# A linear-attention layer and a Fourier-mixing layer in one kernel: the transform in four groups, rows only centred by their sum, the state held in PSUM over three chunks, and the order of all operations given as a table

## The chip, the cores and the metric

The kernel runs on one core of a Trainium2 chip. The metric is the device time of one execution in microseconds. The core has five engines that run side by side, each through its own list of instructions in order: TensorE (PE in the profile, its weight loads PEld), VectorE (DVE), ScalarE (ACT), GpSimd (POOL) and SyncE (SP, which here only starts DMAs). An engine that meets an instruction whose input is not there waits, and everything behind that instruction waits too.

## The reference

There are 4 batches, 8 heads, 768 time steps and a head size of 48, so a row is 8 x 48 = 384 wide.

```python
for t in range(S):                                   # attention with a decaying state
    y[t]  = r[t] . (state + (u * k[t]) v[t]^T)
    state = w * state + k[t] v[t]^T
X = real(fft(fft(x, axis=1), axis=2))                # over 768 steps, then over 384 columns
u = x + X
un = (u - mean(u)) / sqrt(var(u) + 1e-6)             # per row
out = u + relu(un @ w1) @ w2                         # 384 -> 1536 -> 384
```

## The kernel before, in words

The 24 **chunks** (4 batches of 6) have 128 time steps each. For a chunk, SP starts three loads (`k` and `r` into the two halves of `kr`, L306 and L309; `v` into `vt`, L313). DVE scales `k` and `r` by tables of powers of `w` into `KR` (L329), ACT casts `v` to `V` (L334), PE turns `KR` by eight transposes (`tp`, L339), ACT copies that to `KRT` (L342), DVE makes the products `PR` (L343). PE computes the scores `A_ps` (L353); they are masked to `MA` either by ACT (copy `AC`, L365) and POOL (L367) or by DVE alone (L360). The **state** update is PE's `u_ps` (L381): four products of `KR` and `V`, and from the second chunk of a batch on one more product with the identity that adds the previous state `Sst` (L384); DVE multiplies it by `w` to the 128th power, `WD`, into the next `Sst` (L388). The chunk's output gathers in `yd_ps` (L403, L408, L423); the term with `u` goes through ACT (`DE`, L413) and POOL (`TT`, L414), and DVE adds both into the batch's rows `X` (L427).

When a batch's six chunks are there, DVE **folds** it: sums and differences of the two halves of the sequence (`EO`, L445) and of the two halves of the row (`XF`, L451). PE multiplies by the tables of the first transform (L475: 18 products, 384 or 386 columns wide, in six accumulations), ACT copies the result to `TT` (L482; the trace calls it TT as well), DVE copies it reversed to `TR` (L491), which serves the other half of the frequencies. The second transform (L510, L512, L514) takes for each of six blocks of 128 rows six products: two of 384 and four of 192 columns. DVE adds `X` into `UF` (L520), takes each row's mean and variance (L525, L527), ACT and DVE turn these into `rstd` and `nm` (L536 to L540), and ACT writes the normed row `UN` (L545). `UN` is turned into `UNT`, in batch 0 by PE and DVE (L566, L569), in the others by a transposing DMA. The two-layer product follows for each half batch: 12 groups of 3 matmuls (L594) with a relu on ACT into `HT` (L598), then for each block 12 matmuls (L610), and DVE adds `UF` into `osb` (L617), which POOL sends out (L620).

The order in which each engine meets its work is made by a planner in the kernel's Python: every operation is recorded with an engine and a duration in `op`, and `order` starts again and again the operation that can begin first. What comes out is a fixed list for each engine. Until a planned time `WARM` it also puts in products with a tile of zeros (L626), which compute nothing that is used. Tables for the transforms come over SP's queue (`te`, `to`, `hid`, L296), the weights `W1`, `W2` over POOL's (L648).

Of the kernel before, what the change touches and what calls it, by code (L numbers as in the profile page):

```python
# [15 lines left out]
B = 4  # L16
# [7 lines left out]
NP = H // 2  # L24


def _tables():

    bf = mybir.dt.np(BF16)
    n = np.arange(384)  # L30
    ke = np.arange(0, 385, 2)
    ko = np.arange(1, 384, 2)

    def seq(k):
        a = 2.0 * np.pi * np.outer(n, k) / S
        t = np.concatenate([np.cos(a), np.sin(a)], axis=1)
        return t.reshape(3, 128, -1).transpose(1, 0, 2)

    te = seq(ke)
    to = seq(ko)  # L40
    te[:, :, 193] = 0.0
    te[:, :, 385] = 0.0
    d = np.arange(192)
    le = np.arange(0, 384, 2)
    lo = np.arange(1, 384, 2)
    hid = []
    for f, sg in ((np.cos, 1.0), (np.sin, -1.0), (np.sin, 1.0)):
        e = sg * f(2.0 * np.pi * np.outer(d, le) / DM)
        o = sg * f(2.0 * np.pi * np.outer(d, lo) / DM)
        t = np.zeros((128, 768))  # L50
        t[:, 0:192] = e[0:128]
        t[0:64, 192:384] = e[128:192]
        t[64:128, 384:576] = o[0:64]
        t[:, 576:768] = o[64:192]
        hid.append(t)
    hid = np.stack(hid, axis=1)
    mtri = np.triu(np.ones((128, 128)), 1)
    ident = np.eye(128)
    return [np.ascontiguousarray(x.astype(bf)) for x in (te, to, hid, mtri, ident)]


class _Tile:


    def __init__(self, source, ring, bufs):
        self.source, self.ring, self.bufs = source, ring, bufs
        self.ops = []
        self.value = None
# [5 lines left out]
class _Schedule:  # L74

    LATENCY = 80  # L80
    LANDING = 1900
    COLD = 8000

    def __init__(self):
        self.ops, self.made, self.at = [], {}, {}
# [4 lines left out]
    def given(self, name, at):  # L90
        self.at[name] = at

    def op(self, eng, ns, fn, r=(), w=(), new=(), use=(), after=(), dma=0, pri=0, until=None):
        o = dict(eng=eng, ns=ns, fn=fn, deps=list(r), after=list(after), w=list(w), new=list(new), dma=dma, pri=pri, until=until,
                 n=len(self.ops))
        for t in set(new) | set(use):
            t.ops.append(o)
        self.ops.append(o)

    def order(self):  # L100
        makes = {}
        for o in self.ops:
            for k in o["w"]:
                makes[k] = o
        users = {}
        for o in self.ops:
            srcs = {makes[k]["n"] for k in o["deps"] if k in makes}
            behind = {makes[k]["n"] for k in o["after"]} - srcs
            o["left"] = len(srcs) + len(behind)
            o["ready"] = max([0] + [self.at[k] for k in o["deps"] if k in self.at])  # L110
            for n in srcs:
                users.setdefault(n, []).append((o, True))
            for n in behind:
                users.setdefault(n, []).append((o, False))
        free, rings, dma_free, done = {}, {}, 0.0, []
        cand = {}
        for o in self.ops:
            if o["left"] == 0:
                cand.setdefault(o["eng"], []).append(o)

        def room(o):
            t = 0.0
            taken = {}
            for tl in o["new"]:
                ring = rings.setdefault(tl.ring, [])
                n = len(ring) + taken.get(tl.ring, 0) - tl.bufs
                taken[tl.ring] = taken.get(tl.ring, 0) + 1
                if n >= 0:
                    if n >= len(ring):
                        return None  # L130
                    for p in ring[n].ops:
                        if "end" not in p:
                            return None
                        t = max(t, p["end"])
            return t

        total = sum(o["until"] is None for o in self.ops)
        while sum(o["until"] is None for o in done) < total:
            best = None
            for e, ops in cand.items():  # L140
                at = free.get(e, 0.0)
                pick = None
                ops[:] = [o for o in ops if o["until"] is None or at < o["until"]]
                for o in ops:
                    t = room(o)
                    if t is None:
                        continue
                    start = max(at, o["ready"], t + self.LATENCY)
                    key = (start, o["pri"], o["n"])
                    if pick is None or key < pick[0]:  # L150
                        pick = (key, o)
                if pick and (best is None or pick[0] < best[0]):
                    best = pick
            assert best, "no operation can start"
# [35 lines left out]
def kernel(  # L190
# [272 lines left out]
    def fourier(b):  # L463
# [22 lines left out]
        for cb in range(3):  # L486
            for par in range(2):
                first(cb, par)
# [208 lines left out]
```

## Time and profile before

| | |
|---|---|
| time, median of 3 runs | 205.12 us (205.09 to 205.95) |
| profiled execution, its own time | 207.08 us |
| span of the profile, first to last instruction | 205.4 us |
| PE busy / DVE / ACT / POOL | 186.4 / 137.8 / 128.8 / 62.9 us |
| granted TensorE clock, mean | 0.968 |
| filler products with zeros (L626) | 79 in the trace, 21.9 us busy |
| first matmul of the two-layer product (L594) | at 56.81 us |
| last matmul | ends at 200.1 us |

Busy time counts a matmul from its issue to its modelled end; matmuls overlap, so the pace of a run of them is read from their starts. Idle time of an engine costs nothing by itself; what matters is which wait ends last in a stage.

### The profile page before, as it was taken

How to read it: one execution, taken by the hardware profiler on the slowest of the kernel's cores; microseconds unless marked ns; L12 is line 12 of the kernel's file. 1: busy time of each engine (PE TensorE's matmuls, PEld its weight loads, DVE VectorE, ACT ScalarE, POOL GpSimd, SP SyncE). 2: the span in 40 equal slices, each digit the busy share in tenths (PEclk: the TensorE clock that was granted, in tenths of full speed). 3: DMA queues.
4: the chain of work that ended last, by engine and by line, in shares of the span. 5: the costliest groups of instructions: out<-in, count | busy, mean ns of one | idle time of the engine just before them, and what ended most of it. 6: DMA issues, size and time to landing. Idle time of an engine off the chain costs nothing.

```text
span 205.4 us, 4458 instructions
## 1 busy us (share of the span) xinstructions
PE 186.4 (91%) x1737; PEld 117.8 (57%) x1738; DVE 137.8 (67%) x281; ACT 128.8 (63%) x260; POOL 62.9 (31%) x92
## 2 busy tenths in 40 slices
PE   7499955599989997999999999999999999999990
PEld 2256632267566664675677677666657665656650
DVE  5278993859899869998999998983645822111220
ACT  2588640563779795759489895996465585664300
POOL 5035974123023442221456321135311012011131
PEclk9999996759999999999999999999999999999997
DMA  4999999999999769561999200144111045111121
GB/s 100 174 185 172 174 290 256 169 190 182 184 201 169 151 135 202 128 118 38 165 234 204 57 3 0 41 96 96 41 38 38 5 97 130 41 66 53 38 87 66
DMA packets 86549, 24.74 MB, mean 120 GB/s; under 512 B 82944, under 2 KB 84608, under 8 KB 86528
## 3 DMA queue, kind: packets, MB, share of 16 engines
q1 hardware_dynamic: 81664, 16.98, 46.6%
q0 software_dynamic: 3680, 7.08, 13.5%
q10 hardware_dynamic: 1184, 0.39, 0.9%
q8 instruction: 13, 0.21, 0.4%
q14 instruction: 8, 0.07, 0.1%
HBM read 20.32 MB, written 4.72 MB: 122 GB/s over the span
## 4 chain that ended last, share of the span: by engine, by line
PE 41%; issue 25%; DVE 11%; DMA 7%; SPq 7%; POOL 4%; ACT 1%; POOLq 0%; DVEq 0%; ACTq 0%
PE mm L594 9%; PE mm L610 8%; DMA kr<-in_r_dram 7%; PE mm L475 4%; PE tp L339 4%; DVE KR L329 4%; POOL out_dram L620 4%; PE mm L510 3%; PE A_ps L353 2%; PE mm L626 2%; SPq L296 2%; PE mm L514 1%; PE mm L512 1%; PE yd_ps L423 1%; SPq L306 1%
## 5 line engine op out<-in xcount | busy, mean ns | idle before, releaser
L598 ACT ACTIVATE HT<-mm 128x384 bf16<-128x384 f32 x96 | 45.3, 495 | 20.4 <-PE mm L594 20.3
L594 PE MATMUL mm<-UNT,W 128*128 128x384 bf16 x288 | 53.2, 326 | 0.1
L610 PE MATMUL mm<-W,HT 128*128 128x384 bf16 x288 | 50.6, 326 | 0.0
L610 PEld LDWEIGHTS <-HT 128*128 128x128 bf16 x288 | 27.7, 98 | 18.3 <-issue 0.3
L594 PEld LDWEIGHTS <-W 128*128 128x128 bf16 x288 | 26.8, 98 | 16.1 <-issue 0.2
L617 DVE TENSOR_TENSOR osb<-mm,UF 128x384 f32<-128x384 f32 x24 | 13.3, 556 | 32.7 <-PE mm L610 32.7
L367 POOL TENSOR_SCALAR_AFFINE_SELECT MA<-AC 128x512 bf16<-128x512 bf16 x29 | 21.6, 750 | 43.9 <-ACT AC L365 33.9
L620 POOL DMA_DIRECT2D out_dram<-osb x24 | 13.4, 559 | 65.5 <-DVE osb L617 52.2
L329 DVE TENSOR_TENSOR KR<-kr,wtab 128x768 bf16<-128x768 f32 x24 | 26.6, 1106 | 9.2 <-DMA kr<-in_r_dram 9.2
L414 POOL TENSOR_TENSOR TT<-V,DE 128x384 bf16<-128x384 bf16 x24 | 21.7, 905 | 28.0 <-ACT DE L413 27.9
L342 ACT COPY KRT<-tp 128x1024 bf16<-128x1024 bf16 x24 | 24.4, 1018 | 4.1 <-PE tp L339 4.0
L626 PE MATMUL mm<-zero 128*128 128x512 bf16 x79 | 21.9, 404 | 1.3 <-DVE icol L267 1.3
L365 ACT CAST AC<-A_ps 128x512 bf16<-128x512 f32 x29 | 16.5, 588 | 7.6 <-PE A_ps L353 7.4
L339 PE MATMUL tp<-ident,KR 128*128 128x128 bf16 x192 | 15.2, 224 | 6.2 <-DVE KR L329 6.0
L334 ACT CAST V<-vt 128x384 bf16<-128x384 f32 x24 | 11.8, 519 | 12.3 <-DMA vt<-in_v_dram 9.0
L339 PEld LDWEIGHTS <-KR 128*128 128x128 bf16 x192 | 11.9, 100 | 11.3 <-DVE KR L329 9.9
L482 ACT CAST TT<-mm 128x386 bf16<-128x386 f32 (+1 forms) x24 | 12.7, 597 | 6.3 <-PE mm L475 6.3
L545 ACT ACTIVATE UN<-UF,nm,rstd 128x384 bf16<-128x384 f32 x24 | 15.3, 697 | 0.9 <-DVE nm L540 0.9
L427 DVE TENSOR_TENSOR X<-yd_ps,TT 128x384 bf16<-128x384 f32 x24 | 13.1, 547 | 3.9 <-POOL TT L414 3.9
L343 DVE TENSOR_TENSOR PR<-KRT 128x512 bf16<-128x512 bf16 x24 | 13.6, 569 | 1.8 <-ACT KRT L342 1.7
L360 DVE TENSOR_TENSOR MA<-A_ps,mtri 128x512 bf16<-128x512 f32 x19 | 12.9, 680 | 2.6 <-PE A_ps L353 2.5
L520 DVE TENSOR_TENSOR UF<-mm,X 128x384 f32<-128x384 f32 x24 | 12.6, 552 | 1.5 <-PE mm L514 0.6
(67 smaller groups left out, 240.0 us busy)
## 6 DMA issues: line engine op xcount, KB each, us to landing
kr<-in_k_dram SPq DMA_DIRECT2D x24, 192.0 KB, 4.8
vt<-in_v_dram SPq DMA_DIRECT2D x24, 192.0 KB, 4.5
out_dram<-osb POOLq DMA_DIRECT2D x24, 192.0 KB, 2.2
kr<-in_r_dram SPq DMA_DIRECT2D x23, 192.0 KB, 4.4
W<-in_moe_w_ch_dram POOLq DMA_DIRECT2D x6, 384.0 KB, 6.7
hid_t<-hid_c SPq DMA_DIRECT2D x1, 576.0 KB, 9.2
te_t<-te_c SPq DMA_DIRECT2D x1, 289.5 KB, 9.2
to_t<-to_c SPq DMA_DIRECT2D x1, 288.0 KB, 8.2
```

What stands on the lines that cost most here:

```text
L329: op("DVE", 960, lambda: nc.vector.tensor_tensor(out=KR().rearrange("t s p (a d) -> t (s p) a d", a=2)[:, :, :, 0:D], in0=kr().rearrange(" ...
L339: nc.tensor.transpose(tp()[:, s, p, :], KR()[:, s, p, :], ident)
L342: op("ACT", 1010, lambda: nc.scalar.copy(KRT(), tp()), r=[("tp", i)], w=[("KRT", i)], new=[KRT], use=[tp], pri=pri)
L365: op("ACT", 590, lambda: nc.scalar.copy(AC(), A_ps[a]()), r=[("A", i)], w=[("AC", i, a)], new=[AC], use=[A_ps[a]], pri=pri)
L367: op("POOL", 680, lambda: nc.gpsimd.affine_select(out=MA[a](), in_=AC(), pattern=[[0, NP], [1, 128]], base=0, channel_multiplier=-1, compa ...
L414: op("POOL", 850, lambda: nc.gpsimd.tensor_tensor(out=TT(), in0=V(), in1=DE().unsqueeze(2).to_broadcast([128, H, D]), op=AluOp.mult), r=[( ...
L545: op("ACT", 705, lambda: nc.scalar.activation(out=UN()[:, j, :], in_=UF()[:, j, :], func=Act.Identity, scale=rstd()[:, j:j + 1], bias=nm() ...
L594: nc.tensor.matmul(hp(), lhsT=W1[:, dt, ft * 128:(ft + 1) * 128], rhs=UNT()[:, :, dt, :], start=(dt == 0), stop=(dt == 2))
L598: op("ACT", 490, lambda: nc.scalar.activation(out=HT()[:, ft, :], in_=hp(), func=Act.Relu), r=[("hp", hf, ft)], w=[("HT", hf, ft)], new=[H ...
L610: nc.tensor.matmul(mo(), lhsT=HT()[:, ft, j * 128:(j + 1) * 128], rhs=W2[:, ft, :], start=(ft == 0), stop=(ft == 11))
L620: op("POOL", 550, lambda: nc.gpsimd.dma_start(out=out[b, row:row + 128, :], in_=osb()), r=[("osb", hf, j)], w=[("out", hf, j)], use=[osb], ...
L626: op("PE", 216, lambda: nc.tensor.matmul(z(), lhsT=zero[:, 0:128], rhs=zero, start=True, stop=True), r=["zero"], w=[("idle", len(sch.ops)) ...
```

## The change

**The first transform in four groups.** The row is folded once more: after `EO` there is a fold of the row's halves (`HH`) and then a fold of each half onto itself reversed (`XF`, now four groups of 97 columns, stored 98 apart). The first transform has four accumulations, one for each group. For batches 1 to 3 each is three pairs of products of 193 columns. Batch 0 skips the fold of the sequence: each chunk is folded by itself (`narrow`), and each group accumulates six pairs as the chunks come, with a table of opposite sign, `tn_t`, which ACT makes from `te_t`. The second transform has four products of 192 columns for a block, with 97 rows of weights.

**Rows only centred.** The add of `X` also gives the row's sum (`sm`). The turned row is `UB`, which is the row's sum less 384 times the row, so minus 384 times the centred row: it waits for the sum and not for the variance. The factor 384 and the sign are taken back by a relu of the negative and by `rstd` computed for the variance times 384 squared; `osb` multiplies by `rstd` at the end. `nm` and the normed row are gone.

**State in PSUM.** `u_ps` stays for three chunks and each adds its products to it; the tables `wtab` have three versions so that no multiplication by a power of `w` falls between. After the third chunk DVE multiplies by `w` to the 384th power, and only the fourth chunk adds an old state by the identity. The other states are plain copies, on DVE (multiplied by a table of ones and zeros) or on ACT (two copies of half the rows each).

**A stored order.** The planner is gone. `ORDER` lists the numbers of the operations as they are issued; a suffix `.1` takes the operation's other form. Such forms exist for copies (ACT or DVE), the masks (ACT and POOL, or DVE), the rows `X` and `UF` (the added tile is put in by PE through the identity, then ACT copies) and the relu (DVE). The numbers given with `op` are not used any more when the kernel is built.

The counts of instructions that change most:

| | before | change |
|---|---|---|
| first transform, PE | 72 of 384 or 386 columns | 120 of 193 |
| second transform, PE | 48 of 384, 96 of 192 | 96 of 192 |
| old state by identity, PE, 384 columns | 16 | 4 |
| `TT`, `X` by identity, PE, 384 columns | none | 9, 16 |
| fillers, PE | 80 | 40 |
| `KRT` copies on ACT / DVE | 24 / 0 | 11 / 13 |
| masks on ACT with POOL / DVE | 29 / 19 | 27 / 21 |
| relu on ACT / DVE | 96 / 0 | 75 / 21 |
| rows `X` on DVE / ACT | 24 / 0 | 15 / 9 |
| states on DVE / ACT | 20 / 0 | 8 / 12 (24 halves) |
| `UF` on DVE / ACT | 24 / 0 | 8 / 16 |
| normed or centred rows on ACT / DVE | 24 / 0 | 10 / 14 |

Where rows move, in three places. First SP's queue at the end of batch 0's loads, where the tables of the transform stand. Before:

```order
L306 DMA kr<-in_k_dram 128x8x48
L313 DMA vt<-in_v_dram 128x8x48
L296 DMA te_t<-te_c 128x1158
L296 DMA to_t<-to_c 128x1152
L296 DMA hid_t<-hid_c 128x2304
L309 DMA kr<-in_r_dram 128x8x48
L313 DMA vt<-in_v_dram 128x8x48
```

In the change:

```order
L274 DMA kr<-in_r_dram 128x8x48 x2
L276 DMA vt<-in_v_dram 128x8x48 x2
L262 DMA te_t<-te_c 128x2316
L262 DMA hid_t<-hid_c 128x1152
L270 DMA kr<-in_k_dram 128x8x48
L274 DMA kr<-in_r_dram 128x8x48
```

`te_t`, now with the contents of both tables, is SP's 20th transfer instead of its 21st; the `k` of chunk 6, which stood ahead of the tables, now follows them with its `r`.

Second, ACT's list in the same stage, from the masks of chunk 4 on. Before:

```order
L365 CAST AC<-A_ps 128x512
L413 COPY DE<-yd_ps 128x8
L334 CAST V<-vt 128x384
L342 COPY KRT<-tp 128x1024
L365 CAST AC<-A_ps 128x512
L482 CAST TT_732<-mm 128x386
```

In the change:

```order
L324 CAST AC<-A_ps 128x512
L661 ACTIVATE tn_t<-te_t 128x1158
L415 CAST X<-yd_ps 128x384
L361 CAST Sst_93<-u_ps 64x4x48 x2
L392 COPY DE<-yd_ps 128x8
L415 CAST X<-yd_ps 128x384
L392 COPY DE<-yd_ps 128x8
```

The making of `tn_t`, which needs `te_t`, stands ahead of the copies of `X` for chunks 3 and 4 and of `DE` for chunks 4 and 5. POOL's first slice of `W1` waits for the `X` of chunk 3, its slices of `W2` for the `X` of chunk 5; before, they followed the issue of loads of chunks 7 to 12.

Third, DVE's list from the transform of batch 0 to the turned rows. Before:

```order
L491 COPY TR<-TT_732 128x768 x3
L329 TENSOR_TENSOR KR_85<-kr,wtab 128x16x48
L520 TENSOR_TENSOR UF<-mm,X 128x2x192 x6
L427 TENSOR_TENSOR X<-yd_ps,TT 128x384
L525 BN_STATS st<-UF 128x6
L527 BN_AGGR MV<-st 128x2
```

In the change:

```order
L306 COPY KRT<-tp 128x1024
L514 COPY TR<-TT_740 97x768 x2
L546 SCALAR_TENSOR_TENSOR UF,sm<-mm,X 128x2x192 x4
L577 COPY UNT<-mm 128x384 x2
L559 TENSOR_SCALAR UB<-UF,sm 128x384 x2
L329 TENSOR_TENSOR MA<-A_ps,mtri 128x512
```

Before, three more pairs of statistics, a reciprocal and `nm` lie between the last row shown and the first `UNT`; in the change two `UNT` follow the four `UF` at once, and the statistics stand behind later chunks.

The diff, cut to its core (`...` marks what is left out):

```diff
+CH = 98
...
-    def order(self):
...
+    def emit(self, order):
         counts = {}
-        for o in self.order():
+        for n, a in order:
+            o = self.ops[n]
...
-            o["fn"]()
+            o["alts"][a][3]()
+
+
+ORDER = """
+154 153 194 150 155 168 157 160 162 195 151 161 159 196 169 177 156 188 199 176 174 197 191 175 163 158 200 178 173 170 171 198 180 172 164 201 179
...
 def attend(i):
...
+            if ph == 0:
+                c["u"] = new(ps, [128, NP, 2, D], F32, "u_ps", 1)
+            else:
+                c["u"] = chk[i - 1]["u"]
...
+            again = q == 3
...
-                                     start=(p == 0), stop=(q == 0 and p == NP - 1), skip_group_check=True)
-                if q > 0:
+                                     start=(ph == 0 and p == 0), stop=(p == NP - 1 and not again), skip_group_check=True)
+                if again:
                     nc.tensor.matmul(u_ps(), lhsT=ident, rhs=S(), start=False, stop=True, skip_group_check=True)
...
+            def halves():
+                for a in range(2):
+                    nc.scalar.copy(Sn()[a * 64:a * 64 + 64, :, a, :], u_ps()[a * 64:a * 64 + 64, :, a, :])
...
+        op(("xt", i), "NONE", 0, lambda: None, r=[("TT", i), ("de", i)], w=[("xt", i)], use=[], pri=pri,
+           other=[("PE", 166, False, lambda: nc.tensor.matmul(
+               yd()[:, 0:DM], lhsT=ident, rhs=TT().rearrange("p h d -> p (h d)"), start=False, stop=False,
+               skip_group_check=True))], fixed=True)
...
+    def narrow(q, pri):
+        X, HH, XF = bat[0]["X"], bat[0]["HH"], bat[0]["XF"]
+        e, n = divmod(q, 3)
...
+        def sym(h, alu):
+            grp = (slice(0, 4, 3), slice(1, 3, 1))[h]
+            op(("XF", 0, q, h), "DVE", 230, lambda: nc.vector.tensor_tensor(
+                out=XF()[:, e, n, 0:4 * CH].rearrange("t (g c) -> t g c", g=4)[:, grp], in0=HH()[:, :, e, n, 0:CH],
+                in1=HH()[:, :, e, n, 192:192 - CH:-1], op=alu),
...
-        def first(cb, par):
...
+        def first(g):
+            fp = new(ps, [128, 2, 193], F32, "mm", 3)
+            last = (NQ if b == 0 else 3) - 1
...
+                for par in range(2):
+                    if b:
+                        lhsT, rhs = XF()[:, par, nb], te_t[:, g % 2, nb, par, :]
...
+                    nc.tensor.matmul(fp()[:, par, :], lhsT=lhsT[:, g * CH:g * CH + 128], rhs=rhs,
+                                     start=(nb == 0 and par == 0), stop=(nb == last and par == 1), skip_group_check=True)
...
             def mm():
...
+                for g in range(4):
+                    lo = j * 128
+                    tb = g if g % 2 == 0 or not sh else 4 + g // 2
+                    nc.tensor.matmul(mp()[:, g // 2, :], lhsT=src()[0:97, g, lo:lo + 128], rhs=hid_t[0:97, tb, :],
+                                     start=(g == 0), stop=(g == 3), skip_group_check=True)
...
+            op(("UF", b, blk), "DVE", 700, lambda: nc.vector.scalar_tensor_tensor(
+                out=parity(UF()[:, j, :]), in0=mp(), scalar=1.0,
+                in1=parity(X()[:, blk, :]), op0=AluOp.mult, op1=AluOp.add,
+                accum_out=sm()[:, j:j + 1]),
...
+               other=[("ACT", 700, False, lambda: nc.scalar.activation(
+                   out=parity(UF()[:, j, :]), in_=mp(), func=Act.Identity, accum_out=sm()[:, j:j + 1]))],
...
+            op(("UB", b, blk), "ACT", 610, lambda: nc.scalar.activation(
+                out=UB()[:, j, :], in_=UF()[:, j, :], func=Act.Identity, scale=-float(DM), bias=sm()[:, j:j + 1]),
...
-        def normed(sh, UF, UNT, MV):
...
-        op("DVE", 555, lambda: nc.vector.tensor_tensor(out=osb(), in0=mo(), in1=UF()[:, j, :], op=AluOp.add),
...
+        op(("osb", hf, j), "DVE", 620, lambda: nc.vector.scalar_tensor_tensor(
+            out=osb(), in0=mo(), scalar=rstd()[:, j:j + 1], in1=UF()[:, j, :], op0=AluOp.mult, op1=AluOp.add),
...
-    table("te", te_t, te_c.ap(), 900)
-    table("to", to_t, to_c.ap(), 900)
-    table("hid", hid_t, hid_c.ap(), 1500)
+    table("te", te_t, te_c.ap(), 1600, 2)
+    table("hid", hid_t, hid_c.ap(), 800, 3)
+    op("tn", "ACT", 1150, lambda: nc.scalar.mul(tn_t, te_t[:, :, :, 1, :], -1.0), r=["te"], w=["tn"], pri=40,
...
+    weights("W1", lambda n: w1[n * 128:(n + 1) * 128, :], lambda n: W1[:, n, :], [("X", 3)], 1870, -90)
```

More of the change, by code (lines that the diff above doesn't have):

```diff
@@ L634 @@
+    MASKED = 3
     prelude()
-    load(0)
-    for i in range(1, NC):
+    table("ident", ident, id_c.ap(), 100, -48)
+    table("mtri", mtri, mtri_c.ap(), 100, -20)
+    for i in range(NC):
         load(i)
-    table("te", te_t, te_c.ap(), 900)
-    table("to", to_t, to_c.ap(), 900)
-    table("hid", hid_t, hid_c.ap(), 1500)
+    table("te", te_t, te_c.ap(), 1600, 2)
+    table("hid", hid_t, hid_c.ap(), 800, 3)
+    op("tn", "ACT", 1150, lambda: nc.scalar.mul(tn_t, te_t[:, :, :, 1, :], -1.0), r=["te"], w=["tn"], pri=40,
+       other=[("DVE", 700, True, lambda: nc.vector.tensor_scalar(
+           out=tn_t, in0=te_t[:, :, :, 1, :], scalar1=-1.0, scalar2=None, op0=AluOp.mult))])
```

570 lines of the change are left out of this document (259 added, 311 removed), and 35 rows, old and new, of the table ORDER.

## The prediction

> **What bounds the kernel now.** I read the page first, for the shares and the slices over the span.
>
> ```profile
> PE 186.4 (91%) x1737; PEld 117.8 (57%) x1738; DVE 137.8 (67%) x281; ACT 128.8 (63%) x260; POOL 62.9 (31%) x92
> DVE  5278993859899869998999998983645822111220
> PEclk9999996759999999999999999999999999999997
> ```
>
> A slice is 5.1 us. PE is busy for most of the span, but DVE is near full in slices 5 to 27, and the granted clock sags in slices 7 to 9, so one share says little. The second view cuts the span at 56.81 us, where the first matmul of the two-layer product starts, and at PE's end (columns: length, busy PE, PEld, DVE, ACT, POOL with counts, clock, DMA share, GB/s).
>
> ```profile
> 56.80:200.10 143.30, 141.18 (x1314) 91.91 (x1313) 97.08 (x194) 97.34 (x202) 39.87 (x56) 1.00 0.44 95
> 0.00:56.80 56.80, 45.23 (x423) 25.91 (x425) 40.17 (x87) 31.49 (x59) 22.49 (x35) 0.91 1.09 189
> ```
>
> From 56.8 us PE leaves only 2.1 us of 143.3 unbusy, at full clock: this is a **stage bound by PE**, with DVE close behind it until the last fold. Before it lies a **ramp**, where PE also runs fillers. So the span is T (the first L594) + PE's stage + a tail of 205.4 - 200.1 = 5.3 us.
>
> The ramp is read from PE's and DVE's rows in order of time, with the table's issue on SP and the weights' on POOL.
>
> ```profile
> 31.61 0.48 PE L475 MATMUL mm<-te_t,XF 128*128 128x386 bf16 x1 [2.68 <-DMA te_t<-te_c]
> 37.32 0.62 PE L339 MATMUL tp<-ident,KR 128*128 128x128 bf16 x8 [2.57 <-DVE KR L329]
> 56.81 1.14 PE L594 MATMUL mm<-UNT,W 128*128 128x384 bf16 x6
> ...
> 22.32 1.66 SPq L296 DMA_DIRECT2D te_t<-te_c  x1
> ...
> 20.84 0.60 POOL L648 DMA_DIRECT2D W<-in_moe_w_ch_dram  x1
> ...
> 36.31 0.96 DVE L329 TENSOR_TENSOR KR<-kr,wtab 128x768 bf16<-128x768 f32 x1 [3.72 <-DMA kr<-in_r_dram]
> 37.18 0.55 DVE L427 TENSOR_TENSOR X<-yd_ps,TT 128x384 bf16<-128x384 f32 x1
> 46.83 3.46 DVE L520 TENSOR_TENSOR UF<-mm,X 128x384 f32<-128x384 f32 x6
> 55.21 0.36 DVE L569 COPY UNT<-mm 128x384 bf16<-128x384 bf16 x1 [0.52 <-PE mm L566]
> ```
>
> The last X of batch 0 (37.18) stands behind a KR that waits for its load; the table, issued at 22.3, lands 9.3 us later beside weights issued from 20.8; and between the end of the six UF (50.3) and the first turned copy (55.2) lie 4.9 us of statistics and norming. 19.6 us pass from that X to the first L594.
>
> **PE's stage, term by term.** The pace of matmuls comes from the chain of waits and, for narrow ones, from PE's starts in time.
>
> ```profile
> 81.82 1.48 PE mm L475 x9
> ...
> 99.30 0.18 PE u_ps L384
> ...
> 110.14 0.33 PE A_ps L353 x8
> ...
> 111.06 0.45 PE tp L339 x8
> ...
> 45.60 0.33 PE L510 MATMUL mm<-hid_t,TT 128*128 128x384 bf16 x1
> 45.76 0.25 PE L512 MATMUL mm<-hid_t,TT 128*128 128x192 bf16 x1
> 45.85 0.25 PE L514 MATMUL mm<-hid_t,TT 128*128 128x192 bf16 x1
> 45.93 0.33 PE L510 MATMUL mm<-hid_t,TT 128*128 128x384 bf16 x1
> ```
>
> 384 columns take 0.164 us (1.48 / 9), 192 columns 0.083 (45.76 to 45.93, two of them), a block of the second transform twice 0.33 = 0.66. Now what stands behind the first L594 in each kernel, from the two lists:
> - second transform, 18 blocks: 11.9 us becomes 72 x 0.083 = 6.0, plus 14 identity products that add X, 2.3: -3.6.
> - first transform, 3 batches: 54 x 0.164 = 8.9 becomes 72 x 0.083 = 6.0: -2.9.
> - old state by identity, 11 to 3: -1.3; TT by identity, 4 new: +0.7.
> - one more chunk's transposes and scores lie behind the cut: +0.8.
>
> Sum -6.3 (-3.6 - 2.9 - 1.3 + 0.7 + 0.8), so PE's stage is 143.3 - 6.3 = **137.0 us**, if its stalls stay as they are. The 40 fillers that go lie ahead of the cut and fill waits; removing them costs nothing except through the clock (below).
>
> A row for the weight loads:
>
> ```profile
> L339 PEld LDWEIGHTS <-KR 128*128 128x128 bf16 x192 | 11.9, 100 | 11.3 <-DVE KR L329 9.9 <-issue 0.3
> ```
>
> Eight transposes with eight such loads take 0.45 us, 0.056 a pair, so loads overlap and a pair of load and 192 columns holds 0.083. If loads could not overlap each other, the 216 narrow products would take 100 ns each, 3.7 us more in all; the transposes speak against that. The Trainium skill ("TensorE: Matmul & The Clock Gate", LDWEIGHTS) puts a load of 128 columns at 128 / 1.2 = 107 ns; by it the same case would cost 5.2 us, an estimate, and the transposes' 56 ns speak against it as well.
>
> **DVE beside it.** Costs come from the page and the groups by line.
>
> ```profile
> L329 DVE TENSOR_TENSOR KR<-kr,wtab 128x768 bf16<-128x768 f32 x24 | 26.6, 1106 | 9.2 <-DMA kr<-in_r_dram 9.2
> L414 POOL TENSOR_TENSOR TT<-V,DE 128x384 bf16<-128x384 bf16 x24 | 21.7, 905 | 28.0 <-ACT DE L413 27.9
> L342 ACT COPY KRT<-tp 128x1024 bf16<-128x1024 bf16 x24 | 24.4, 1018 | 4.1 <-PE tp L339 4.0
> L343 DVE TENSOR_TENSOR PR<-KRT 128x512 bf16<-128x512 bf16 x24 | 13.6, 569 | 1.8 <-ACT KRT L342 1.7
> L360 DVE TENSOR_TENSOR MA<-A_ps,mtri 128x512 bf16<-128x512 f32 x19 | 12.9, 680 | 2.6 <-PE A_ps L353 2.5
> L520 DVE TENSOR_TENSOR UF<-mm,X 128x384 f32<-128x384 f32 x24 | 12.6, 552 | 1.5 <-PE mm L514 0.6
> L569 DVE COPY UNT<-mm 128x384 bf16<-128x384 bf16 x6 | 1.9, 345 | 0.5 <-PE mm L566 0.5
> L617 DVE TENSOR_TENSOR osb<-mm,UF 128x384 f32<-128x384 f32 x24 | 13.3, 556 | 32.7 <-PE mm L610 32.7
> L525 DVE BATCH_NORM_STATS2 st<-UF 128x6 f32<-128x384 f32 x24 | 12.8, 532 | 0.1
> L598 ACT ACTIVATE HT<-mm 128x384 bf16<-128x384 f32 x96 | 45.3, 495 | 20.4 <-PE mm L594 20.3
> L413 ACT COPY DE<-yd_ps 128x8 f32<-128x8 f32 x24 | 4.0, 169 | 6.8 <-PE yd_ps L423 5.3 <-PE yd_ps L408 1.2
> ...
> 78.73 2.06 DVE L451 TENSOR_TENSOR XF<-EO 128x1152 bf16<-128x1152 bf16 x2
> 114.26 2.37 DVE L451 TENSOR_TENSOR XF<-EO 128x1152 bf16<-128x1152 bf16 x2
> ```
>
> Forms that the trace lacks get bounds from their neighbours. KRT on DVE (1024 from PSUM, bf16): 0.67 to 0.92; from 384 to 512 columns in fp32 the rows rise 1 ns a column, the bf16 copy should rise half that, 345 + 640 x 0.5 = 0.67; the other end is L569's time by length. UF with its sum: 0.55 (L520) to 0.9 (L520 and another copy), I take 0.65, on either engine. The scaled osb: 0.55 to 0.7, I take 0.60. Relu on DVE: 0.55 (L617's size). UB on DVE, an fp32 tile in SBUF: 0.35 to 0.55, I take 0.35.
>
> Between the folds that end at 80.8 and 116.6 the rows of DVE's list add up to 38.5 us by mean durations, and took 35.8: a factor of 0.93, since consecutive instructions overlap. In the change DVE has, from the first turned copy to batch 3's last fold, 112 us by such a list (16 KR 17.7, 17 PR 9.7, 12 masks 8.2, 18 statistics 12.8, 18 relus 9.9, 15 osb 9.0, 13 X 7.1, folds 17.4, the rest 20): 104 us at 0.93. PE's useful work in the same piece of its list is 100 us, 103.5 with the share of stalls that it has now. **Both engines end level**, so PE's stage keeps 137 us only if neither makes the other wait; I add 1 us and carry up to 7 as the unknown.
>
> **The ramp.** The table is SP's 20th transfer instead of its 21st, so it is issued near 21.5. Its weights' neighbours go: the first slice of W1 now waits for X of chunk 3, which stands on ACT behind tn, which needs the table. Landing lies between a load's usual time and today's:
>
> ```profile
> kr<-in_k_dram SPq DMA_DIRECT2D x24, 192.0 KB, 4.8
> ```
>
> 21.5 + 4.8 = 26.3 and 31.6; I take 28.5, as it has three times the bytes. Then ACT makes tn (1158 columns at L342's ns a column, 1.2 us), X 0.5, two half states 0.7, DE 0.2; POOL TT 0.9; PE and X of chunk 4 0.9; DE and TT of chunk 5 1.1; DVE's X 0.55 and four small folds of batch 0, 1.4: 36 us. SP's queue: the loads of chunk 6 follow the tables and lie ahead of the weights, so KR is ready. DVE's list then has KR 1.1, the copy of TT, PR, mask and KRT 2.5, two TR 0.8, four UF 2.6, two UNT 0.7: 7.7, so 43.7; the second transform on PE (6 x 0.33) and UB (0.35 on DVE, ACT as L520) wait on each other in between, some 2 us. **T = 46**, with 42 (table at 26.3, no waits) and 53 (table as late as now, and half clock) as bounds. The statistics, 4.9 us today, move behind the first L594, under PE's stage and onto DVE's count above. W1, issued near 30 to 33, must have landed by T.
>
> The span: 46 + 137 + 1 + 5.3 = 189.3. The profiled execution's own time is 207.08, 1.7 above its span; the median of the runs is 205.12, 0.3 below the span. So **189 us**.
>
> **Clock.** Today's waits of 2.7 and 2.6 us on PE are followed by
>
> ```profile
> 32.00:34.00 2.00, 1.86 (x21) 1.26 (x21) 0.58 (x2) 0.17 (x1) 0.00 (x0) 0.50 1.21 245
> ```
>
> a granted clock of 0.50 (next to last columns: clock, DMA share, GB/s). Half of the fillers go; if PE again waits so long for the table, batch 0's 48 narrow products take 8 us instead of 4. The Trainium skill ("TensorE: Matmul & The Clock Gate", The HAM clock gate) states that a gap of about 3.4 us halves the clock; here 2.7 was enough, and the measurement decides.
>
> **The rivals.**
> - *The ramp does not shrink*: the table or W1 lands as late as today, tn holds ACT, PE runs at half clock. T = 53 to 56; 196.5 to 199.5. For it: loads are saturated to 60 us (DMA share 1.09). Against: the weights leave the table's way. 0.12.
> - *DVE decides*: its new forms cost the upper bounds (13 KRT +3, 24 osb +2, UB +2), PE waits at folds. 193 to 196. 0.16.
> - *Neither waits*: T = 43, no extra stalls, 136: 181 to 185. For it: PE stalls only 2 us now. 0.10.
> - *Weight loads set the pace of narrow matmuls*, 100 ns each: 189 + 3.7 = 192.7. Against it the 56 ns above. 0.02.
> - *Slower: the state's single buffer.* PE stands at each u_ps until the copy of the last state has left the same bank, and on ACT that copy is queued behind relus. The gain is 16 us and there are 20 updates, so it decides from 0.8 us of PE's wait an update; at 1 us it gives 209. Against it: today PE's update also needs the previous state and shows no such wait. 0.04.
>
> That the change doesn't turn rows earlier is not open: UB needs only the sum.
>
> **Chances.** The forecast, 185 to 193, has 0.56. For 8 in 10 the range takes in DVE's case and parts of the ramp's and the best case: 181.5 to 197, leaving out about 0.15. Differences under 0.5%, 1 us, cannot be told here from none. Faster: 0.94 (all but the slower rival and a little); same 0.02; slower 0.04.
>
> **What would show it.** First L594 near 46 (above 52: the ramp is wrong); te_t landing near 28; no clock of 0.5 over more than one stage of 2 us; from the first L594 to PE's end 136 to 140; narrow products 0.083 apart; no wait of PE's u_ps on a state above 0.3; DVE above 95% up to the third fold. I am wrong if PE's stage is above 144 or T above 53.

## The result

The change takes 198.78 us (median of 4 runs, 198.48 to 199.51) against 205.53 for the kernel before beside it (4 runs, 205.09 to 207.26): a ratio of 0.9662, 95% interval 0.9598 to 0.9726. It is **faster by 3.4%**. The forecast was 189.0 with a range of 181.5 to 197: the direction was right, the size was not, and the time lies above the range. Medians here are of all executions; a ratio and its interval leave out those over 1.5% longer than the fastest of their kernel.

The profiled execution took 198.48 us by its own time, with a span of 196.4. The page's first lines:

```profile
span 196.4 us, 4461 instructions
PE 170.4 (87%) x1711; PEld 113.8 (58%) x1711; DVE 148.6 (76%) x334; ACT 112.2 (57%) x263; POOL 60.5 (31%) x90
DVE  7789994167889998989898979998888969702140
PEclk9999999669999999999999999999999999999999
```

PE's busy share fell and DVE's rose. The seventh to ninth slices (4.9 us each) stand out: DVE falls to 4 and then 1 tenth in the seventh and eighth, the clock to 6 tenths in the eighth and ninth. The span is cut as the prediction cut it, at the first L618 (the L594 of before) and at PE's end (columns: stretch, length, busy PE, PEld, DVE, ACT, POOL with counts, clock, DMA share, GB/s).

```profile
0.00:49.42 49.42, 34.57 (x390) 23.40 (x391) 36.20 (x99) 27.19 (x60) 16.34 (x27) 0.93 1.03 192
49.42:191.12 141.70, 135.86 (x1323) 90.44 (x1322) 111.76 (x235) 85.04 (x204) 43.60 (x62) 1.00 0.45 103
```

So T went from 56.8 to 49.4, PE's stage from 143.3 to 141.7, and the tail stayed at 5.3 us. Against the forecast (T 46, stage 138 with its 1 us of stalls) T is 3.4 too long and the stage 3.7. In the stage PE is without work for 5.8 us (141.70 - 135.86), where it was 2.1 before.

The ramp, from the rows in order of time of PE, ACT and POOL:

```profile
37.68 0.48 PE L403 MATMUL yd_ps<-V,MA 128*128 128x48 bf16 x8 [6.21 <-ACT V L296]
49.42 0.65 PE L618 MATMUL mm<-UNT,W 128*128 128x384 bf16 x3
52.39 0.25 PE L381 MATMUL yd_ps<-UW,PR 128*128 128x2 bf16 x4 [1.67 <-DVE PR L307]
...
25.58 0.46 ACT L415 CAST X<-yd_ps 128x384 bf16<-128x384 f32 x1
37.12 1.13 ACT L296 CAST V<-vt 128x384 bf16<-128x384 f32 x2 [7.60 <-DMA vt<-in_v_dram]
...
25.36 0.60 POOL L671 DMA_DIRECT2D W<-in_moe_w_ch_dram  x1
27.64 1.14 POOL L671 DMA_DIRECT2D W<-in_moe_w_ch_dram  x2
38.49 2.29 POOL L671 DMA_DIRECT2D W<-in_moe_w_ch_dram  x3
```

The weights do not wait for rows of `X`, as I had said ahead of the result: the first slice of `W1` starts at 25.36, before ACT's copy of `X` of chunk 3 (25.58), and those of `W2` at 38.49, before DVE's `X` of chunk 5 (38.57). `weights` still names these rows, but only the planner that is gone read such names; in the built kernel a slice stands where `ORDER` has it on POOL's list, the first one behind `TT` of chunk 3 and a mask.

PE stands for 6.2 us before `y` of chunk 5, since ACT cannot make that chunk's `V`. The chain of waits gives the loads behind it (start, length, what):

```profile
19.37 5.11 DMA te_t<-te_c
24.50 1.17 ACT tn_t L661
25.89 11.20 DMA vt<-in_v_dram
40.48 11.14 DMA vt<-in_v_dram
```

The table, whose landing was my worry, landed at 24.5. What came late is `v` of chunks 5 and 7: issued at 25.89, 11.2 us to land, beside the three slices of `W1` issued from 25.36 to 28.8. SP's stored list has `v` of chunk 6 ahead of that of chunk 5. The same happens again at 40.48 beside the slices of `W2` (issued 38.5 to 40.8): that load is the `v` of chunk 9, whose cast stands on DVE ahead of `PR`, for which PE waits at 52.39. The usual times of such transfers are shorter (KB each, median us to landing):

```profile
vt<-in_v_dram SPq DMA_DIRECT2D x24, 192.0 KB, 3.9
W<-in_moe_w_ch_dram POOLq DMA_DIRECT2D x6, 384.0 KB, 7.6
```

After the gap PE works at half clock until past 42 us (stretches of 2 us, clock third from the end):

```profile
36.00:38.00 2.00, 0.32 (x9) 0.32 (x9) 0.00 (x0) 0.77 (x2) 0.29 (x1) 0.50 0.59 119
40.00:42.00 2.00, 2.00 (x18) 1.92 (x17) 1.05 (x2) 1.06 (x2) 0.78 (x2) 0.50 1.17 161
42.00:44.00 2.00, 2.00 (x25) 1.58 (x24) 1.50 (x3) 1.62 (x4) 0.00 (x0) 0.80 1.27 200
```

Behind T the longest waits of PE are these:

```profile
PE mm L618 <- DMA UNT<-UB: 2.6, 3, 1.2
PE yd_ps L381 <- DVE PR L307: 1.7, 1, 1.7
```

The first comes once a batch, when the turned rows of the batch's first half come over the transposing DMA. So there were two questions: whose fault the ramp's hole is, and what sets the stage.

### The profile page after: what moved, and what is told of

It reads as the page before. It is cut to its first block, busy times and chain, and to the rows that moved or that the text cites. A ratio compares the mean times of both kernels' runs of the same rounds, so it can differ in the third digit from the quotient of the medians.

```text
span 196.4 us, 4461 instructions
## 1 busy us (share of the span) xinstructions
PE 170.4 (87%) x1711; PEld 113.8 (58%) x1711; DVE 148.6 (76%) x334; ACT 112.2 (57%) x263; POOL 60.5 (31%) x90
## 3 DMA queue, kind: packets, MB, share of 16 engines
q1 hardware_dynamic: 81520, 16.69, 43.8%
## 4 chain that ended last, share of the span: by engine, by line
PE 49%; DMA 20%; issue 19%; POOL 3%; DVE 3%; ACT 2%; SPq 1%; POOLq 0%; DVEq 0%
PE mm L618 15%; PE mm L638 14%; DMA vt<-in_v_dram 11%; PE tp L302 5%; DMA UNT<-UB 3%; DMA kr<-in_r_dram 3%; PE mm L495 3%; PE A_ps L317 3%; DMA te_t<-te_c 3%; POOL out_dram L650 2%; PE yd_ps L403 2%; PE mm L533 2%; PE u_ps L349 1%; PE yd_ps L386 1%; DVE KR L290 1%
## 5 line engine op out<-in xcount | busy, mean ns | idle before, releaser
L618 PE MATMUL mm<-UNT,W 128*128 128x384 bf16 x288 | 53.5, 326 | 2.6 <-DMA UNT<-UB 2.6
L638 PE MATMUL mm<-W,HT 128*128 128x384 bf16 x288 | 51.0, 326 | 0.0
L623 ACT ACTIVATE HT<-mm 128x384 bf16<-128x384 f32 x75 | 36.4, 492 | 18.1 <-PE mm L618 18.0
L638 PEld LDWEIGHTS <-HT 128*128 128x128 bf16 x288 | 27.2, 98 | 16.8
L618 PEld LDWEIGHTS <-W 128*128 128x128 bf16 x288 | 26.0, 97 | 18.3 <-DMA UNT<-UB 3.1
L650 POOL DMA_DIRECT2D out_dram<-osb x24 | 13.4, 557 | 48.6 <-DVE osb L646 45.0
L326 POOL TENSOR_SCALAR_AFFINE_SELECT MA<-AC 128x512 bf16<-128x512 bf16 x27 | 18.3, 684 | 25.2 <-ACT AC L324 13.9
L646 DVE SCALAR_TENSOR_TENSOR osb<-mm,rstd,UF 128x384 f32<-128x384 f32 x24 | 14.8, 615 | 12.8 <-PE mm L638 12.3
L626 DVE TENSOR_SCALAR HT<-mm 128x384 bf16<-128x384 f32 x21 | 11.6, 554 | 9.8 <-PE mm L618 9.5
L198 PE MATMUL mm<-zero 128*128 128x512 bf16 x40 | 12.6, 416 | 6.8 <-DVE eps_t L231 6.8
L412 DVE TENSOR_TENSOR X<-yd_ps,TT 128x384 bf16<-128x384 f32 x15 | 8.3, 553 | 8.5 <-POOL TT L394 6.8
L305 ACT COPY KRT<-tp 128x1024 bf16<-128x1024 bf16 x11 | 11.1, 1013 | 5.5 <-PE tp L302 5.3
L403 PE MATMUL yd_ps<-V,MA 128*128 128x48 bf16 x192 | 8.8, 184 | 6.2 <-ACT V L296 6.2
L495 PE MATMUL mm<-te_t,XF 128*128 128x193 bf16 x108 | 13.4, 261 | 0.5 <-DVE XF L433 0.5
L403 PEld LDWEIGHTS <-MA 128*128 128x128 bf16 x192 | 8.2, 97 | 9.7 <-issue 7.3
```

Of the source, the lines that this page charges most:

```text
L326: op(("MA", i, a), "POOL", 630, lambda: nc.gpsimd.affine_select(out=MA[a](), in_=AC(), pattern=[[0, NP], [1, 128]], base=0, channel_multip ...
L403: nc.tensor.matmul(y[:, h, :], lhsT=MA[a]()[:, p, :], rhs=V()[:, h, :], start=False, stop=(h == H - 1), skip_group_check=True)
L495: nc.tensor.matmul(fp()[:, par, :], lhsT=lhsT[:, g * CH:g * CH + 128], rhs=rhs, start=(nb == 0 and par == 0), stop=(nb == last and par == ...
L618: nc.tensor.matmul(hp(), lhsT=W1[:, dt, ft * 128:(ft + 1) * 128], rhs=UNT()[:, :, dt, :], start=(dt == 0), stop=(dt == 2))
L623: op(("HT", hf, ft), "ACT", 495, lambda: nc.scalar.activation(out=HT()[:, ft, :], in_=hp(), func=Act.Relu, scale=-1.0), r=[("hp", hf, ft)] ...
L638: nc.tensor.matmul(mo(), lhsT=HT()[:, ft, j * 128:(j + 1) * 128], rhs=W2[:, ft, :], start=(ft == 0), stop=(ft == 11))
```

## The experiments

Each edit is to the change unless it says otherwise. Edits of the order are shown as the list of the engine that issues the operation, with chunks as numbers.

### The late loads moved ahead of the weights

```diff
 SP:   k6 r6
+SP:   v5 v7
 SP:   k7 r7
-SP:   v5 v7
 SP:   k8 r8
```

> The loads of v for chunks 5 and 7 stand ahead of k and r of chunk 7 in SP's queue, so ahead of the weights; nothing else moves. Theory A (the ramp lost its time because these two loads, issued at 25.89 beside three slices of W1 issued 25.36 to 28.8, took 11.2 us to land): they land by 29, PE's 6.21 us wait before y of chunk 5 (37.68) goes below 1 us, no slice at half clock after it, first L618 at 41 to 44 in place of 49.42, time 191 to 194. Rival B (loads are saturated to 60 us, so what is put earlier only makes others late): a wait of the same size stands at KR or V of chunk 7 to 9, first L618 at 47 or later, time 196.5 to 199. Rival C (tn on ACT and what hangs on it is the cause): y of chunk 5 stays later than 33.

Measured: 199.73 us, ratio to before 0.9671 (0.9616 to 0.9726); against the change no difference can be told. T was 51.12. From PE, DVE and SP in order of time:

```profile
43.84 1.03 PE L302 MATMUL tp<-ident,KR 128*128 128x128 bf16 x8 [6.29 <-DVE KR L290]
...
42.83 0.96 DVE L290 TENSOR_TENSOR KR<-kr,wtab 128x768 bf16<-128x768 f32 x1 [7.62 <-DMA kr<-in_r_dram]
...
29.67 0.70 SPq L274 DMA_DIRECT2D kr<-in_r_dram  x1
```

`y` of chunk 5 no longer waits, but `r` of chunk 7, now issued at 29.7 behind the `v`, takes 13 us (29.67 to 42.8) and PE stands for 6.3 us there. The slices of `W1` are issued from 25.3 to 30.1 there, those of `W2` from 32.2, so this load runs beside both. **The hole has moved, not gone**: rival B, though the time lies 0.7 above its range, and the place of the two loads alone was not the cause.

### `W1` later

```diff
-POOL: TT3 W1[1] TT4 W1[2] W1[0] TT5 W2[1] W2[0] W2[2]
+POOL: TT3 TT4 TT5 W1[1] W1[2] W1[0] W2[1] W2[0] W2[2]
```

> The three slices of W1 are issued behind TT of chunk 5 on POOL, in place of behind TT of chunks 3 and 4; the loads keep their order. Theory A: without the weights beside them the two loads of v issued near 25.9 land in 4 to 6 us (31 to 32) in place of 11.2, y of chunk 5 starts at 32 to 33; W1 is issued near 32.5 to 34 and lands 7 us later, near 40, so the first L618 comes at 43 to 47 and the time is 193 to 197. Rival (SP's own queue is backed up, the weights are innocent): landing stays above 9 us, the first L618 comes at 49 or later, time 198 to 201.

Measured: 201.50 us, 0.9772 (0.9732 to 0.9812), slower than the change and outside theory A's 193 to 197. Yet the first half of theory A held: `v` of chunk 5 landed in 4.85 us and T was 43.36. Then (PE's wait and first L638, DVE, POOL, and the two loads in the chain of waits):

```profile
52.63 0.27 PE L381 MATMUL yd_ps<-UW,PR 128*128 128x2 bf16 x4 [7.95 <-DVE PR L307]
67.15 1.14 PE L638 MATMUL mm<-W,HT 128*128 128x384 bf16 x6
...
51.88 0.36 DVE L297 CAST V<-vt 128x384 bf16<-128x384 f32 x1 [8.47 <-DMA vt<-in_v_dram]
...
32.68 3.93 POOL L671 DMA_DIRECT2D W<-in_moe_w_ch_dram  x6
...
26.09 4.85 DMA vt<-in_v_dram
34.26 17.59 DMA vt<-in_v_dram
```

All six weight slices now go out from 32.7 on, and the hole stands at `v` of chunk 9, which takes 17.6 us beside them. That is a waste: `W2` is first read at 67 us and takes its share of the transfers from 33 us on. Both runs together fit DMA engines that are full (a share of 0.97 to 1.04 up to T in each variant of the change in this section), so that a move only chooses who is late. It led to the next theory, D: what must move is what is not needed yet.

### `W1` and `W2` later, and `W2` alone

For the first, as above and `W2` behind `TT` of chunk 7:

```diff
-POOL: TT5 W1[1] W1[2] W1[0] W2[1] W2[0] W2[2] TT6 MA6 MA7 TT7 MA8
+POOL: TT5 W1[1] W1[2] W1[0] TT6 MA6 MA7 TT7 W2[1] W2[0] W2[2] MA8
```

> As e2_w1_late, and the three slices of W2 behind TT of chunk 7 on POOL, in place of right behind W1. Theory D (the loads share the DMA engines with weights that are not needed yet: W2 is first used at 64.6 us but was issued at 38.5 to 40.8, and the 8 us hole of e2_w1_late at V of chunk 9 is W2's share): v of chunk 9 lands by 42 in place of 51.9, the 7.95 us wait before PR goes below 1 us, first L618 at 41 to 43.5, W2 lands before 60 and the first L638 comes at 57 to 61; time 189 to 194. Rival B (the sum of bytes up to some point sets the time, and a hole of 6 to 8 us only moves on, now to the first L638 behind W2 or to the loads of chunks 10 to 12): time 197 to 202.

For the second, `W2` alone:

```diff
-POOL: TT5 W2[1] W2[0] W2[2] TT6 MA6 MA7 TT7 MA8
+POOL: TT5 TT6 MA6 MA7 TT7 W2[1] W2[0] W2[2] MA8
```

> The change with W2 alone behind TT of chunk 7; W1 stays where it was. Theory D: the wait of 6.21 us before y of chunk 5 stays (it is W1's), the two loads of v issued at 40.48 land in 5 us in place of 11.1, PE's wait of 1.7 us before PR (52.39) goes; W2 lands in time for the first L638 (64.6); time 196.5 to 198. Rival B: W2 is late for L638 by 3 us or more: time above 200.

Measured: **192.83 us**, 0.9365 (0.9327 to 0.9403), with both late; 197.48, 0.9627 (0.9570 to 0.9684), with `W2` alone. With both late, the stretches up to T and behind it, PE's first L618 and first L638, and a piece of the chain:

```profile
0.00:43.77 43.77, 32.26 (x387) 21.56 (x390) 37.66 (x101) 27.87 (x61) 15.92 (x25) 1.00 0.98 195
43.77:184.54 140.77, 135.89 (x1322) 90.46 (x1322) 110.03 (x232) 84.36 (x202) 45.24 (x64) 1.00 0.51 110
...
43.77 0.66 PE L618 MATMUL mm<-UNT,W 128*128 128x384 bf16 x3 [1.50 <-DMA W<-in_moe_w_ch_dram]
58.05 1.14 PE L638 MATMUL mm<-W,HT 128*128 128x384 bf16 x6
...
26.48 4.31 DMA vt<-in_v_dram
34.31 10.73 DMA vt<-in_v_dram
```

There is no hole and no half clock up to T (1.00); the first L638 comes at 58 and does not wait for `W2`. T is now set by `W1` (1.5 us of wait). `v` of chunk 9 still takes 10.7 us beside `W1` and lands at 45, not by 42 as I had expected, but it costs PE only 0.7 us. With `W2` alone late, the wait of 6.15 us before `y` stays, which is `W1`'s, and the one before `PR` is gone (0.8 us remain at the same product, for a relu on ACT):

```profile
37.38 0.48 PE L403 MATMUL yd_ps<-V,MA 128*128 128x48 bf16 x8 [6.15 <-ACT V L296]
```

In the main theory D held in both, and rival B fell: the bytes that waited until they were needed cost PE little later, the 1.5 us before T.

### The loads in the order in which they are used

To the kernel with both weights late:

```diff
-SP:   v6 v4 te hid k6 r6 k7 r7 v5 v7 k8 r8 v11 v8 k10 r10 v9 v10 k9 r9 k11 r11
+SP:   v5 v4 te hid k6 r6 k7 r7 v6 v7 k8 r8 v8 k9 r9 v9 v10 k10 r10 k11 r11 v11
```

and on ACT the casts of `V` of chunks 5 and 6 change places.

> As e4_w1_w2_late, and the loads of chunks 8 to 11 on SP in the order in which DVE and ACT take them (8, 9, 10, 11 in place of v11, v8, k10, r10, v9, v10, k9, r9, k11), and chunks 5 and 6 change places for v (load and bf16 copy). Theory D: no wait for a load above 1 us up to 60 us, y of chunk 5 at 29 to 31, no half clock, first L618 at 40 to 42.5 set by W1's landing; time 187 to 191. Rival B: as for e4_w1_w2_late, 197 to 202. If it is no better than e4_w1_w2_late, the order among the loads is worth nothing once the weights are out of the way.

Then chunks 5 and 6 alone, load and cast, with the other loads as the change has them:

```diff
-SP:   v6 v4 te hid k6 r6 k7 r7 v5 v7
+SP:   v5 v4 te hid k6 r6 k7 r7 v6 v7
```

> As e4_w1_w2_late, and chunks 5 and 6 change places for v alone (load and bf16 copy), without the other order of the loads of chunks 8 to 11 that e6_order_of_need had. If the better part of e6_order_of_need was the early v of chunk 5 (first L618 at 43.04, no wait for W1) and its worse part the order of the later loads (stage 144.1 against 140.8), then the first L618 is at 42.3 to 43.3, the stage 140.5 to 141.5, the time 191 to 192.5. If the early v of chunk 5 itself makes later loads late, the stage is above 143 and the time 193.5 to 195.5.

Measured: 194.15 us, 0.9398 (0.9324 to 0.9473), and 193.45, 0.9363 (0.9313 to 0.9413): neither can be told from 192.83. The stages of the second:

```profile
0.00:41.77 41.77, 31.33 (x386) 21.07 (x390) 36.88 (x99) 26.94 (x60) 14.69 (x24) 1.00 0.98 194
41.77:185.27 143.50, 136.05 (x1323) 90.42 (x1322) 111.41 (x235) 85.15 (x204) 45.33 (x65) 1.00 0.55 111
45.45 0.25 PE L381 MATMUL yd_ps<-UW,PR 128*128 128x2 bf16 x4 [2.37 <-DVE PR L307]
```

T comes 2.0 us earlier and the stage is 2.7 longer: what the early `v` wins is lost again, 1.7 of it before `PR` (a wait of 2.4 for 0.7) and 0.6 before `KR`. The full order of need did the same (T 43.04, stage 144.1). My guess that the later loads' order was the bad part of it was wrong; the second case came, with a stage above 143. Once the weights are out of the way, neither of these two orders of the loads is worth anything that can be seen.

### The state afresh at each chunk

```diff
-            if ph == 0:
-                c["u"] = new(ps, [128, NP, 2, D], F32, "u_ps", 1)
-            else:
-                c["u"] = chk[i - 1]["u"]
+            c["u"] = new(ps, [128, NP, 2, D], F32, "u_ps", 1)
-            again = q == 3
+            again = q > 0
```

> Undoes one part of the change: the state starts anew in PSUM at every chunk and the old one is added by an identity product in each (15 such products in place of 4 in all four batches, less the first chunk of each); same order of all else. If PE bounds its stage, 12 more products of 384 columns at 0.164 us cost 2.0 us, 1.6 of them behind the first L618: time 200.3 to 201. If DVE or ACT decides the stage, they fill PE's waits and the time rises by less than 0.5 us: 198.5 to 199.3. If fresh starts make PE wait for the copies of the state, u_ps waits of 0.5 us and more an update show up and the time is above 203.

Measured: 202.13 us, 0.9831 (0.9758 to 0.9904), 3.4 above the change. T was 49.56; the stage:

```profile
49.56:194.68 145.12, 137.13 (x1331) 91.09 (x1330) 112.05 (x235) 85.01 (x204) 44.26 (x62) 1.00 0.48 101
136.09 2.61 PE L615 MATMUL mm<-UNT,W 128*128 128x384 bf16 x15 [2.73 <-DMA UNT<-UB]
```

PE's work rises by 1.3 (137.13 - 135.86), its waits by 2.1, nearly all at the end of batch 2; no `u_ps` waits for a state copy. The time lies in none of the three expected ranges: 1.1 above that of PE as the bound. The state kept in PSUM is worth 3.4 us in this order, of which its products explain 1.3; and my slower rival, PE standing at each update, is wrong for this order. Of the wait of 2.73 us, which is 0.62 in the change, 1.7 is the transposing DMA itself: it lands 4.90 us after its issue at 131.15, and 3.22 in the change. Why it takes longer is not shown.

### DVE loaded and relieved

The statistics done twice:

```diff
-op(("st", b, blk), "DVE", 550, lambda: nc.vector.bn_stats(out=st(), in_=UF()[:, j, :]), ...
+def stats():
+    for _ in range(2):
+        nc.vector.bn_stats(out=st(), in_=UF()[:, j, :])
+op(("st", b, blk), "DVE", 550, stats, ...
```

> The change with every bn_stats on DVE (24, 0.53 us each) done twice: 12.8 us more on DVE, nothing on PE. If DVE and PE end level behind the first L618, as I forecast, DVE's 9.5 us up to the third fold (18 of them) lengthen the stage by 6 to 9 us: 205 to 208. If PE decides and DVE (76% busy) has slack, the time rises by 0 to 2.5 us: 199 to 201.

The other way, on the kernel with both weights late, the 18 relus of the first six halves that stood on DVE take their ACT form, in the same places (`.1` struck from 18 numbers of `ORDER`):

> As e4_w1_w2_late (192.83; stage behind the first L618 140.8, of it 4.9 without PE at work), and the 18 relus on DVE ahead of the last batch's halves go to ACT in the same places of the list: DVE loses 10.0 us (18 x 0.554), ACT gains 8.9 (18 x 0.492). Theory E (DVE's sum of work sets the stage, as 12.8 us more of it lengthened it by 7.5): PE's waits for the transposing DMA, for X and for KR shrink, stage 136 to 139, time 188 to 191. Rival F (the chain at each batch's end sets it, folds, transform, UF, UB, transposing DMA, in which DVE and ACT are both full, and relus lie elsewhere): stage 140 to 142, time 192 to 194; above 194 ACT's queue has become the bound.

Measured: 206.40 us, 1.0035 (0.9994 to 1.0076), with the statistics twice; 191.22, 0.9292 (0.9243 to 0.9340), with the relus on ACT. The stages of both, and a stretch of the first behind a batch's end:

```profile
49.22:198.40 149.18, 138.77 (x1323) 91.05 (x1322) 122.60 (x259) 85.47 (x204) 43.98 (x62) 0.99 0.43 97
135.93 3.28 PE L622 MATMUL mm<-UNT,W 128*128 128x384 bf16 x11 [1.68 <-DMA UNT<-UB]
136.00:138.00 2.00, 2.00 (x7) 0.97 (x8) 0.51 (x1) 0.55 (x2) 0.20 (x1) 0.50 0.00 0
```

```profile
42.82:183.88 141.06, 135.99 (x1322) 90.59 (x1322) 101.89 (x215) 90.30 (x220) 45.49 (x64) 1.00 0.51 110
85.84 1.64 PE L618 MATMUL mm<-UNT,W 128*128 128x384 bf16 x9 [0.80 <-DMA UNT<-UB]
```

The second statistics take 13.4 us by their durations and raise DVE's busy time in the stage by 10.8 (122.60 - 111.76). They lengthen the stage by 7.5: 4.6 of waits and 2.9 of slower work, part of it at half clock. Of the waits, 1.1 is again a transposing DMA that took longer, 4.28 us in batch 2 for 3.22. The 18 relus, 10 us of DVE's work by their durations, stood in other places; without them the stage is where it was (141.06 against 140.77), with the same waits for `UNT`. The first result is what "level" foretold, the second is not: theory E falls, and rival F's stage came. So DVE's sum alone does not set the stage. But ACT took over 8.9 us by their durations in the same move, so it is not shown that relief of DVE which loads no other engine would be worth nothing. That it is the chain at a batch's end (folds, transform, `UF`, `UB`, transposing DMA) fits the waits that stay, but no run shortened that chain, so it is argued and not shown. The kernel with the relus on ACT is the fastest measured, but by its interval hardly to be told from the one without. Its profile has an earlier T (42.82), and 0.35 of the 1.6 us between the two medians lies outside the span: time less span is 1.7 in its four runs and 2.0 to 2.1 in the four of the other.

### The kernel before, for its spans

> The kernel before, unchanged, for its spans. If the profiled execution of before (span 205.4, own time 207.08) was a slow one, the spans of the other executions are 1.6 to 2.1 us below their own times, so near 203.3 for times near 205.1, and the prediction's step from span to median (0.3 below the span) was wrong by 2 to 2.5 us. If own time and span are apart by different amounts from run to run (0 to 2 us), that step was as good as could be had.

Measured: 206.35 us, ratio to itself 0.9975 (0.9937 to 1.0013), 10 runs from 204.11 to 208.38. Its spans were for example 203.8, 204.5 and 202.4 us for times of 205.51, 206.24 and 204.11: time less span is 1.7 to 1.8 in all ten. In the change's four runs it is 2.0 to 2.1. The profile of the run of 205.51 has the same stage as the one that the forecast started from, 143.3 us, and a T of 55.2 in place of 56.8: that the first profile was a long one lay in its ramp.

## Why the prediction was wrong, step by step

The forecast missed by 9.8 us: 3.4 in T, 3.7 in PE's stage, 2.7 from span to time.

**The ramp (3.4 us).** Two steps failed. The sum from the table to 36 us has no term for `V` of chunk 5. Among the loads I looked only at `k` and `r`, and there "so KR is ready" held: `KR` of chunk 6 (30.83) does not wait for its load. I did not look at `v`, and PE stood for 6.2 us because `v` of chunk 5 took 11.2 to land. And "W1, issued near 30 to 33" was issued from 25.36, beside that `v`: the table landed at 24.5 and not at 28.5, and the first slice does not wait for `X` of chunk 3. I took the removal of the weights from beside the table as their removal; they went on to the next transfers. With `W1` issued from 32.7 or 33.0, `v` of chunk 5 lands in 4.9 or 4.3 us and T is 43.4 or 43.8, below my 46. I had saturated loads as a point for the rival that the ramp does not shrink; the mechanism was there, and I let it act on the table alone. The clock step held: "if PE again waits so long" it runs at half clock, and it did.

**PE's stage (3.7 us).** The sum of removed work was near: 5.3 us (141.18 - 135.86) for 6.3, so 1.0 of the miss is here; which of its terms was short stays open. The term that failed is "I add 1 us" for stalls: PE's time without work went from 2.1 to 5.8, 2.7 more than forecast. Of the 5.8, 1.7 is the late `v` of chunk 9, so the ramp again, and 2.6 the transposing DMA at three batches' ends. "Both engines end level" was half right. Up to the end of the third fold:

```profile
49.42:157.60 108.18, 103.50 (x1104) 69.81 (x1103) 97.11 (x198) 69.96 (x169) 39.28 (x54) 1.00 0.53 116
```

DVE is busy for 90% of that stretch, not over 95%. More on DVE cost time; less elsewhere on it, with more on ACT, gave none. I compared two sums, and the waits for the transposing DMA at a batch's end, 2.6 us here and none in the profile before, were in none of my terms. What sets that end, where everything depends on the last `X`, stays open, as said above.

**From span to time (2.7 us).** I set the median of before 0.3 below the span of an execution that was itself 2 us slower than the median. Time less span is 1.7 to 1.8 in all of before's executions; 198.78 lies 2.4 above the change's profiled span, 2.1 as time less span and 0.3 because the profiled execution was the fastest. A forecast of a span should have got the 1.7; why the change has 0.3 to 0.4 more is not shown.

**What held.** The price of each new form, from the groups by line (busy, mean ns):

```profile
L306 DVE COPY KRT<-tp 128x1024 bf16<-128x1024 bf16 x13 | 8.9, 686 | 2.6 <-PE tp L302 2.5
L559 DVE TENSOR_SCALAR UB<-UF,sm 128x384 bf16<-128x384 f32 x14 | 6.0, 466 | 0.1
L546 DVE SCALAR_TENSOR_TENSOR UF<-mm,X 128x384 f32<-128x384 f32 x8 | 4.4, 554 | 0.7 <-PE mm L533 0.7
L546 DVE DVE_READ_ACCUMULATOR UF<-mm,X 128x1 f32 x8 | 0.7, 83 | 0.0
L552 ACT ACTIVATION_READ_ACCUMULATOR UF<-mm 128x1 f32 x16 | 3.0, 190 | 0.0
```

`KRT` 0.69 for 0.67, `UF` with its sum 0.64 for 0.65, and `UB` 0.47 in the mean (0.40 to 0.79 one by one), inside its bounds of 0.35 and 0.55 but not at the end I took. The narrow products ran at the pace of 0.083 us:

```profile
30.89 0.25 PE L495 MATMUL mm<-tn_t,XF 128*128 128x193 bf16 x1
30.97 0.25 PE L495 MATMUL mm<-te_t,XF 128*128 128x193 bf16 x1
```

so weight loads did not set it. The relu (0.554), `osb` (0.615) and `tn` (1.17) came as taken. No `u_ps` waited for a state behind T; ahead of it one did, for 0.64 us.

**The chances.** Faster at 0.94 was right. The time fell into the range of the rival whose ramp does not shrink (196.5 to 199.5, 0.12), but not for its reason: it took T as 53 to 56 with the stage as forecast, and T was 49.4, so that range was met by luck; late loads and half clock came true in part. Of DVE deciding (193 to 196, 0.16) PE's waits at a batch's end came, but not the upper prices of the new forms. I had no case for a part of each together, and that is what was measured.

## What to carry to other kernels

Where the DMA engines are full, cost a moved transfer by what then runs beside it, for every load in the same stretch and not only for the one that was late before, and look first for bytes that are fetched long before they are read: moving 6 slices of weights was worth 6 us here, two other orders of the loads among themselves nothing. Read from the list that is built, not from a dependency that is only named, when a transfer will start. Two engines whose sums are level can both have idle time; that a single chain through both at a batch's end is the reason is argued here and not shown, but count such a chain by itself. And take span and time from the same execution.

## What the runs showed of the hardware that I had not expected

- A load of 192 KB that usually lands in 3.9 us took 11.2 beside three slices of weights, and 13.1 and 17.6 beside slices of both weights (`r` of chunk 7 with the two `v` moved, `v` of chunk 9 with `W1` later). Up to T the change and its variants moved 190 to 198 GB/s at a DMA share of about 1, whatever the order.

```profile
DMA packets 86404, 24.43 MB, mean 124 GB/s; under 512 B 82928, under 2 KB 84592, under 8 KB 86384
```

  Nearly all packets are under 512 bytes; a head's row is 48 floats, 192 bytes. The Trainium skill ("DMA: Bandwidth & Descriptors", Specifications) gives 512 bytes as the least transfer for full rate and a fabric ceiling of 435 GB/s. The rate here lies far below that, but no run changed the packets, so that this is the reason is not shown.
- An operation that also gives a row's sum is two instructions: the accumulator is read by one of its own, 0.08 us on DVE and 0.19 on ACT, as the rows above show.
- The length of a wait of PE alone does not tell whether the clock falls. A wait of 1.68 us with the statistics twice (PE busy for 0.32 of the 2 us from 134 to 136, for 1.38 of the 2 before) was followed by a stretch at clock 0.50, and in the kernel before one of 2.7. The wait of 1.67 us that ends at 52.39 in the change (0.72 of the 2 us from 50 to 52, 1.82 of the 2 before) was not, and neither was that of 2.73 us with the state afresh: the stretches of 2 us in it and behind it have clock 1.00. What decides is not shown.
- The transposing DMA of a half batch lands 3.2 to 3.6 us after its issue in the change. With the state afresh it took up to 4.9; no run shows why.
